# Three layers in one kernel on one core: the experts' second product is written with features as rows

## The chip, the cores and the metric

The kernel runs on one core of a Trainium2 chip. Its time is the device time of that core in microseconds (us). A core has five engines with queues of their own: PE (TensorE, the matrix array), DVE (VectorE), ACT (ScalarE), POOL (GpSimd) and SP (SyncE, which here only issues DMAs). Each works off its instructions in the order in which they were written; a wait on another engine holds up everything behind it on the same engine. PSUM, the memory that PE writes, has eight banks; one bank holds 128 rows of 512 float32.

## The reference

Three layers follow each other. Only the last is touched by the change.

```python
# 1. linear attention (4 batches, 8 heads, 768 steps, head width 48) -> x [3072, 384]
# 2. x = (h * tanh(softplus(h))) @ w_out,  h = x @ w_in        (384 -> 2048 -> 384), the "mish layer"
# 3. a mixture of 8 experts, all of them on every token:
P = exp(x @ w_gate - max)                 # [3072, 8], then 8 rounds of Sinkhorn scaling
for e in range(8):
    h = maximum(x @ w1[e], 0)             # 384 -> 1024
    out += P[:, e:e+1] * (h @ w2[e])      # 1024 -> 384
```

## The kernel before

Tokens are handled in 6 tiles of 512 (`n`), hidden features in chunks of 128 (`f`, 8 of them in an expert). A *unit* is one expert, one tile and one chunk; the experts have 8 x 6 x 8 = 384 units, and a loop passes over them with the expert outermost and the chunk innermost. To reach float32 accuracy at PE's fast rate, each operand is split into a high and a low fp32r part, and every product is taken three times (`PASSES`: high x high, high x low, low x high).

In a unit, `first(i)` (L254) makes the hidden chunk `ph`: 3 parts of x by 3 passes, 9 matmuls that each move 512 token columns past a 128x128 block of weights. `relu(i)` (L322 on ACT, L323 on DVE) turns `ph` into the two parts of `g`. `second_e(j)` (L364) multiplies by w2. Here a block of `g` (128 hidden features x 128 tokens) is loaded as the weights and 384 columns of w2 move: 4 blocks of tokens by 3 passes, 12 matmuls. The sums are four banks `ye`, one for each 128 tokens, with *tokens* as rows. In a loop iteration PE gets `first(i + 1)` and then `second_e(i - 2)`.

After a tile's eighth chunk, the four sums are added to the running result `acc` (L375, DVE, `scalar_tensor_tensor`): since tokens are rows, the expert's weight `P` is one number for each partition. With the last expert, four DMAs write the tile to `out` (L377). `first` products rotate over four PSUM banks (tag `h`), the sums over four others (`y0` to `y3`).

The mish layer before it has units too. There both products are written in the other form (L254 and `second_m`, L334): weights are loaded as weights, and 512 token columns of activations move, 9 matmuls and 9.

The order on every engine is the order of the Python calls (a manual schedule); SBUF and PSUM tiles come from pools that rotate, and an instruction that takes a slot waits for the last reader of the slot's holder before.

Of the kernel before, what the change touches and what calls it, by code (L numbers as in the profile page):

```python
# [21 lines left out]
NP = H // 2          # head pairs  # L22
DD = 2 * D           # columns of a pair
DR = 64 + D          # rows of a pair: the second head's begin at 64
C = 128              # chunk of the recurrence
NC = S // C
NTOK = B * S
DM = H * D           # 384
KI = DM // 128       # 3
TT = 512             # tokens of a tile  # L30
# [8 lines left out]
# square of the upper half of a float64 2^-126, read as a float32, by 2^30  # L39
TINY_SQ = 1.265625  # L40
H_MAX = 12.0
HUGE_SQ = 1.5e10     # no less than the square of the upper half of a float64 2^128
W_MIN, W_MAX = 0.6, 1.0625   # decays that the chunked form takes
ONE_BITS = 0x3F800000
PASSES = ((0, 0), (0, 1), (1, 0))
NWA = 24             # weight pieces of the lasting pool
# [6 lines left out]
NCA = 12             # weight pieces split beside the attention  # L53


@with_exitstack
def fused_kernel(ctx: ExitStack, tc: tile.TileContext, a, out):
    nc = tc.nc
    # the one activation table that holds both exp and ln
    nc.scalar.add_instruction(mybir.InstLoadActFuncSet(  # L60
        name=nc.get_next_instruction_name(), engine=mybir.EngineType.Activation, ins=[], outs=[],
        act_func_set_id=[t.name for t in SETS].index("natural_log_exp_and_others")))
    bad = ctx.enter_context(tc.tile_pool(name="bad", bufs=1)).tile([1, 1], F32, name="bad")
    layers(tc, a, out, bad, False)
    # decays or weights beyond the ranges that the chunked form and the conversion hold for
    with tc.If(nc.values_load(bad.bitcast(I32), min_val=0, max_val=ONE_BITS) > 0):
        layers(tc, a, out, None, True)
# [3 lines left out]
def layers(ctx: ExitStack, tc: tile.TileContext, a, out, bad, general):  # L71
# [9 lines left out]
    def bank(shape, nm, tag):  # L81
        """PSUM: four banks that rotate for first products, four for sums"""
        return ps.tile(shape, F32, name=nm, tag=tag, bufs=4 if tag == "h" else 1)
# [12 lines left out]
    wi, wo, rawn = {}, {}, []  # L96
    # the second product follows the first by some units, and so do its weights
# [17 lines left out]
    def conv_bits(m):  # L115
        """float64 weights, by their bits: the upper 21 bits of the value and the rest, in four steps"""
        load_raw(m + 1)
        lo, hi = rawn[m][:, :, 0], rawn[m][:, :, 1]
        v = mr.tile([128, DM], F32, name=f"v{m}", tag="v")
        q = mr.tile([128, DM], F32, name=f"q{m}", tag="q")  # L120
        parts[m] = v, q
        vb, qb = v.bitcast(U32), q.bitcast(U32)
        # exponent of 11 bits to 8: the top bit and the lower seven; sign, 20 bits of the fraction
        dve.tensor_scalar(vb, hi, 3, 0x3FFFFFFF, op0=ALU.logical_shift_left, op1=ALU.bitwise_and)  # L124
        yield
        dve.scalar_tensor_tensor(vb, hi, 0xC0000000, vb, op0=ALU.bitwise_and, op1=ALU.bitwise_or)  # L126
        yield
        if general:
            # below float32's normal range: zero; above: infinite
            sq = me.tile([128, DM], F32, name=f"sq{m}", tag="e", bufs=MB[0])  # L130
            act.activation(sq, hi.bitcast(F32), AF.Square)
            dve.scalar_tensor_tensor(v, sq, TINY_SQ * 2.0 ** -30, v, op0=ALU.is_ge, op1=ALU.mult)
            dve.tensor_scalar(sq, sq, HUGE_SQ, None, op0=ALU.is_lt)
            dve.reciprocal(sq, sq)
            dve.tensor_tensor(v, v, sq, op=ALU.mult)
        # the lower 32 bits of the fraction
        dve.tensor_scalar(qb, vb, 0xFF800000, None, op0=ALU.bitwise_and)  # L137
        yield
        dve.scalar_tensor_tensor(q, lo, 2.0 ** -52, q, op0=ALU.mult, op1=ALU.mult)  # L139
        yield  # L140

    def conv_act(m):
        # two exact fp32r parts of 24 bits in all
        w, f = wpieces[m]
        t = wA.tile([128, 2, KI, 128], F32R, name=f"wm{m}", tag="w")
        act.activation(t[:, 0].rearrange("p k f -> p (k f)"), parts[m][0], AF.Copy)
        (wi, wo)[w][f] = t
        load_raw(m + 3)
# [18 lines left out]
    def flag(m):  # L167
        # what lies outside float32's normal range leaves a mark
# [5 lines left out]
    # rings that the attention and the layers after it share  # L174
# [50 lines left out]
    # all tiles but the last see one half of the hidden features first, then the other,  # L225
    # so that the weights' parts can follow
# [8 lines left out]
    # weight pieces that are begun beside unit i  # L235
# [22 lines left out]
    def mish_e(i):  # L258
        # e = exp(min(h, H_MAX)), s = (e + 1)^2; beyond, tanh of the softplus is 1 in float32
# [10 lines left out]
    def mish_n(i):  # L270
        # tanh(log1p(e)) = e (e + 2) / (s + 1); what comes out is negative until the sums are taken
# [8 lines left out]
    def mish_r(i):  # L280
        # r = 1 / (s + 1), to be refined
# [6 lines left out]
    def mish_y(i):  # L288
        # ((s + 1) r - 2) r
# [66 lines left out]

    def second_e(j):
        e, n, f = units[j]
# [8 lines left out]
        if f == NF2 - 1:  # L367
            for s in range(NSUB):
                yo, o, gc = sums[n][s], acc[n][:, s, :], n * NSUB + s
                if e == 0:  # L370
                    act.activation(o, yo, AF.Copy)
                    continue
                if e == 1:
                    act.activation(o, o, AF.Copy, scale=Pm[:, gc, 0:1])
                dve.scalar_tensor_tensor(o, yo, Pm[:, gc, e:e + 1], o, op0=ALU.mult, op1=ALU.add)  # L375
                if e == E - 1:
                    nc.sync.dma_start(out[gc * 128:(gc + 1) * 128, :], o)  # L377

# [16 lines left out]
    def gate_out(n, pl):  # L395
        if not g32s or pl is not me:
            g32s.append(pl.tile([32, TT], F32, name=f"g32_{n}", tag="g32"))
            pool.memset(g32s[-1], 0.0)
        g32 = g32s[-1]
        act.activation(g32[0:2 * E, :], gate[n], AF.Copy)  # L400
        gt = pl.tile([32, TT // 32, 32], F32, name=f"gt{n}", tag="y", bufs=MB[3] if pl is me else 1)
        dve.transpose(gt.rearrange("p a b -> p (a b)"), g32)
        gv = gt.rearrange("p (s q) e -> p s q e", q=4)
# [43 lines left out]
    # what comes beside the units: splits of the next tile's x, the gate of a finished tile  # L447
# [21 lines left out]
    # ------------------------------------------------------------------  # L469
    # linear attention: chunks of 128 steps, head pairs stacked on partitions  # L470
    # ------------------------------------------------------------------
    last = []

    def chunked_attention(aw, ac):
# [36 lines left out]
        # power tables of w  # L511
        zero = ac.tile([DR, 1], F32, name="zero")
        pool.memset(zero, 0.0)
        Wr = ac.tile([DR, NP, C], F32, name="Wr")        # w^(j-64)
# [8 lines left out]
        # keeps the array busy, for its clock, until the first scores  # L523
# [3 lines left out]
        Wp = gpl.tile([DR, NP, 192], F32, name="Wp", tag="g")      # w^(j+1)  # L527
# [13 lines left out]
        Wk = ac.tile([DR, NP, C], F32, name="Wk")        # w^(63-j)  # L541
# [7 lines left out]
        def tables():  # L549
            powers(64, 192)  # L550
            Wh = me.tile([DR, NP, C], F32, name="Wh", tag="p", bufs=MB[2])        # w^(191-s)
# [28 lines left out]
        def a_q(i):  # L580
            # u term: b[s, h] = sum_d r u k
# [27 lines left out]
        def a_scores(i):  # L609
            x = T[i]  # L610
            # the two heads of a pair take their own rows of the array and banks
# [57 lines left out]
        def a_cv(i):  # L669
            # half a weight piece beside a unit  # L670
# [10 lines left out]
        # what each engine does while the scores of unit i are made, in its order  # L681
# [26 lines left out]
    def stepwise_attention(ac):  # L708
        """any w: the recurrence as it stands, for one column of the states of a head pair at a time"""
# [4 lines left out]
        # columns e and D + e of sel[:, D - 1 - e:] sum the rows of one head each  # L714
# [57 lines left out]
    with mst, tc.tile_pool(name="hf", bufs=1) as hf:  # L772
# [5 lines left out]
        for i in range(NM + 3):  # L778
            e, n, f = units[i]
            # the first product one unit ahead (two at the start), the second three behind  # L780
# [10 lines left out]
            # units i, i - 1 and i - 2, and between the steps on DVE the bits of a weight piece  # L791
# [42 lines left out]
    cp2 = ctx.enter_context(tc.tile_pool(name="cp2", bufs=1))  # L834
    sk = ctx.enter_context(tc.tile_pool(name="sk", bufs=1))
    acc = [cp2.tile([128, NSUB, DM], F32, name=f"acc{n}") for n in range(NT)]
# [6 lines left out]
    for i in range(NM + 3, NU + 2):  # L843
# [5 lines left out]
        if i < NU:  # L849
# [15 lines left out]
            if bad is not None and e == 2:  # L865
                # the mish layer's weights pass once more, beside the products, to be looked at
# [4 lines left out]
            if bad is not None and e == 3 and n == 0 and f == 2:  # L871
                # 1 for all that is in range; the least of every partition; are there 128 of them?
# [6 lines left out]
                dve.tensor_scalar(bad, okp, 127.5, None, op0=ALU.is_lt)  # L879
            if e == 0:  # L880
                if 0 <= m - 4 < KI:
# [17 lines left out]
def _lay_out(x):  # L899
# [8 lines left out]
    # rows of a head pair on the partitions: 48 of one head, 16 of none, 48 of the other  # L908
    def rows(z, fill=0):
        """z: [head of the pair, d, ...]"""  # L910
# [16 lines left out]
    # row of w_in that a partition of a feature chunk holds  # L927
# [26 lines left out]
```

## Time and profile before

| what | value |
|---|---|
| time, median of 3 runs | 2187.86 us (2185.88 to 2190.61) |
| the profiled execution: its span | 2188.3 us |
| PE busy | 2145.9 us, 98% |
| DVE, ACT, POOL busy | 911.3, 913.2 and 640.3 us |
| attention | about 0 to 155 us |
| mish layer | about 155 to 580 us |
| experts | 580 to 2183 us |

The profile is of one execution. "Busy" counts the time in which at least one instruction of the engine is in flight. PE's instructions overlap (a matmul is some 390 ns in flight, while the next starts 170 to 240 ns after it), so that the distance from start to start, not the duration, tells what a matmul costs. The rows that give this distance are those of the timeline: there neighbouring instructions of one line stand merged, with their count, and the next row's start tells when the group gave way.

### The profile page before, as it was taken

How to read it: one execution, taken by the hardware profiler on the slowest of the kernel's cores; microseconds unless marked ns; L12 is line 12 of the kernel's file. 1: busy time of each engine (PE TensorE's matmuls, PEld its weight loads, DVE VectorE, ACT ScalarE, POOL GpSimd, SP SyncE). 2: the span in 40 equal slices, each digit the busy share in tenths (PEclk: the TensorE clock that was granted, in tenths of full speed). 3: DMA queues.
4: the chain of work that ended last, by engine and by line, in shares of the span. 5: the costliest groups of instructions: out<-in, count | busy, mean ns of one | idle time of the engine just before them, and what ended most of it. 6: DMA issues, size and time to landing. Idle time of an engine off the chain costs nothing.

```text
span 2188.3 us, 27812 instructions
## 1 busy us (share of the span) xinstructions
PE 2145.9 (98%) x10974; PEld 1905.7 (87%) x10974; DVE 911.3 (42%) x1507; ACT 913.2 (42%) x1899; POOL 640.3 (29%) x550
## 2 busy tenths in 40 slices
PE   7889999999999999999999999999999999999998
PEld 7787777788889999999999999999999999999998
DVE  9999999999523322222212222222222122222222
ACT  6889898899522322244432122221311221221111
POOL 5546767655411211131013012211310131121100
PEclk8999999999999999999999999999999999999999
DMA  9640001000100100023311001000100010000000
GB/s 241 191 146 24 30 29 44 15 15 15 31 11 11 33 19 1 12 69 95 97 33 44 1 8 30 22 1 11 48 1 4 12 44 1 8 22 15 15 29 31
DMA packets 42204, 82.51 MB, mean 38 GB/s; under 512 B 5072, under 2 KB 28112, under 8 KB 42064
## 3 DMA queue, kind: packets, MB, share of 16 engines
q1 hardware_dynamic: 42064, 80.64, 12.6%
q8 instruction: 88, 1.44, 0.3%
q14 instruction: 52, 0.43, 0.1%
HBM read 75.91 MB, written 4.72 MB: 37 GB/s over the span
## 4 chain that ended last, share of the span: by engine, by line
PE 85%; DVE 7%; ACT 3%; issue 2%; DMA 1%; POOL 1%; SPq 0%; DVEq 0%; ACTq 0%; POOLq 0%
PE ph L254 41%; PE ye L364 37%; PE x L334 5%; DVE q L137 1%; DVE ph L273 1%; DVE y L292 1%; PE ya L656 1%; DVE q L139 1%; DMA ld<-in_rkT_dram 1%; DVE pn L276 1%; ACT A L607 1%; DMA lt<-in_kr_dram 1%; DVE v L126 0%; DVE y L295 0%; PE ya L654 0%
## 5 line engine op out<-in xcount | busy, mean ns | idle before, releaser
L364 PE MATMUL ye<-we,g 128*128 128x384 f32 x4608 | 869.9, 337 | 0.0
L254 PE MATMUL ph<-xs,we 128*128 128x512 f32 x3456 | 861.9, 393 | 0.0
L364 PEld LDWEIGHTS ye<-we,g 128*128 128x128 f32 x4608 | 819.1, 188 | 34.1 <-DVE xT L350 0.5
L254 PEld LDWEIGHTS ph<-xs,we 128*128 128x128 f32 x3456 | 642.4, 188 | 117.9 <-issue 0.2
L322 ACT ACTIVATE g<-ph 128x512 fp32r<-128x512 f32 x384 | 229.7, 600 | 1137.2 <-PE ye L364 1132.3
L323 DVE SCALAR_TENSOR_TENSOR g<-ph,g 128x512 fp32r<-128x512 f32 x384 | 260.9, 688 | 975.5 <-ACT g L322 975.4
L196 POOL TENSOR_TENSOR xs<-xT,xs 128x512 fp32r<-128x512 f32 x177 | 227.6, 1295 | 866.5 <-ACT xs L195 866.5
L221 POOL TENSOR_TENSOR we<-er,we 128x384 fp32r<-128x384 f32 x118 | 117.7, 1015 | 414.7 <-ACT we L220 414.7
L334 PE MATMUL x<-g,wm 128*128 128x512 f32 x864 | 216.5, 392 | 7.8 <-POOL g L317 7.6
L254 PE MATMUL ph<-xs,wm 128*128 128x512 f32 x864 | 211.9, 390 | 0.6 <-POOL xs L196 0.6
L334 PEld LDWEIGHTS x<-g,wm 128*128 128x128 f32 x864 | 160.5, 188 | 48.3 <-POOL g L317 14.2
L254 PEld LDWEIGHTS ph<-xs,wm 128*128 128x128 f32 x864 | 161.9, 188 | 36.7 <-POOL xs L196 1.1
L375 DVE SCALAR_TENSOR_TENSOR acc<-ye,Pm,acc 128x384 f32<-128x384 f32 x168 | 92.8, 613 | 228.1 <-PE ye L364 228.1
L317 POOL TENSOR_TENSOR g<-y,g 128x512 fp32r<-128x512 f32 x96 | 124.3, 1295 | 134.9 <-ACT g L312 130.8
L195 ACT ACTIVATE xs<-xT 128x512 fp32r<-128x512 f32 x177 | 105.3, 622 | 0.0
L261 ACT ACTIVATE e<-ph,lim 128x512 f32<-128x512 f32 x96 | 65.7, 684 | 35.5 <-DVE pn L276 30.2
L273 DVE TENSOR_TENSOR ph<-ph,e 128x512 f32<-128x512 f32 x96 | 66.6, 694 | 17.2 <-ACT e L263 17.0
L263 ACT ACTIVATE e<-e,lim 128x512 f32<-128x512 f32 x96 | 68.5, 714 | 0.0
L276 DVE SCALAR_TENSOR_TENSOR pn<-e,ph 128x512 f32<-128x512 f32 x96 | 65.8, 685 | 4.3 <-DVE v L124 0.2
L292 DVE SCALAR_TENSOR_TENSOR y<-sq,ph 128x512 f32<-128x512 f32 x96 | 65.2, 679 | 0.0
L656 PE MATMUL ya<-A,vz 128*96 128x128 f32 x384 | 63.4, 298 | 0.0
L220 ACT ACTIVATE we<-er 128x384 fp32r<-128x384 f32 x128 | 61.6, 515 | 1.0 <-DMA er<-in_w_dram 1.0
(118 smaller groups left out, 1295.1 us busy)
## 6 DMA issues: line engine op xcount, KB each, us to landing
er<-in_w_dram SPq DMA_DIRECT2D x128, 192.0 KB, 2.4
ld<-in_rkT_dram SPq DMA_DIRECT2D x24, 448.0 KB, 5.5
lt<-in_kr_dram SPq DMA_DIRECT2D x24, 384.0 KB, 5.8
raw<-in_w_in_dram SPq DMA_DIRECT2D x16, 384.0 KB, 3.1
raw<-in_w_out_dram SPq DMA_DIRECT2D x16, 384.0 KB, 3.0
seen<-in_w_in_dram SPq DMA_DIRECT2D x16, 384.0 KB, 3.1
seen<-in_w_out_dram SPq DMA_DIRECT2D x16, 384.0 KB, 3.0
lv<-in_v_dram SPq DMA_DIRECT2D x24, 192.0 KB, 3.1
```

The lines of the kernel that those rows point to most:

```text
L195: act.activation(xs[:, 0, :], xT[n][:, k, :], AF.Copy)
L196: eng.tensor_tensor(xs[:, 1, :], xT[n][:, k, :], xs[:, 0, :].bitcast(F32), op=ALU.subtract)
L221: eng.tensor_tensor(tl, raw, th.bitcast(F32), op=ALU.subtract)
L254: pe.matmul(ph, w[:, pw, k, :], xs[:, px, :], start=(m == 0), stop=(m == 3 * KI - 1))
L273: dve.tensor_tensor(ph, ph, e, op=ALU.mult)
L276: dve.scalar_tensor_tensor(pn, e, 2.0, ph, op0=ALU.add, op1=ALU.mult)
L317: pool.tensor_tensor(gs[i][:, 1], y, gs[i][:, 0].bitcast(F32), op=ALU.subtract)
L322: act.activation(g[:, 0], ph, AF.Relu)
L323: dve.scalar_tensor_tensor(g[:, 1], ph, 0.0, g[:, 0].bitcast(F32), op0=ALU.max, op1=ALU.subtract)
L334: pe.matmul(sums[n][k], wo[f][:, pw, k, :], g[:, px, :], start=(f == f0 and m == 0), stop=(f == f1 and m == 2))
L364: pe.matmul(sums[n][s], g[:, px, s * 128:(s + 1) * 128], w2[e, f][:, pw].rearrange("p k f -> p (k f)"), start=(f == 0 and m == 0), stop=(f ...
L375: dve.scalar_tensor_tensor(o, yo, Pm[:, gc, e:e + 1], o, op0=ALU.mult, op1=ALU.add)
```

## The change

The second product of the experts takes the form of the mish layer, in 47 of the 48 pairs of expert and tile: blocks of w2 are the weights, 512 columns of `g` move, 3 blocks of output features by 3 passes, 9 matmuls. The sums are three banks with *features* as rows (they rotate over the four banks). Now P differs along the columns. So P is turned once (`p_rows`, two matmuls with the identity), written to DRAM (`prow`), and for every expert and tile 512 values of it are read back into all 128 partitions (`load_p`, tile `pb`).

At the end of a tile, DVE multiplies a sum by `pb` into `t`, and POOL adds `t` to `acc`, three times. (For the second expert POOL also scales `acc` by the first expert's `pb`.) With the last expert each finished third of `acc` is turned in blocks of 32x32 on DVE and goes to `out` in 12 DMAs of 64 KB, whose pieces are 128 bytes.

The last expert's last tile stays in the old form (`second_t`). For it, `acc` of that tile is turned to tokens as rows by 12 matmuls (`turn`), four times three, one group in each of four units of the tile before. A helper of the gate also shares a buffer differently; the remaining differences are comments.

```diff
     def second_e(j):
         e, n, f = units[j]
+        if (e, n) == TOKJ:
+            return second_t(j)
         if f == 0:
-            sums[n] = [bank([128, DM], f"ye{e}_{n}_{s}", f"y{s}") for s in range(NSUB)]
+            sums[n] = [bank([128, TT], f"ye{e}_{n}_{k}", f"y{(ycnt[0] + k) % 4}") for k in range(KI)]
+            ycnt[0] += KI
         g = gs.pop(j)
-        for s in range(NSUB):
+        for k in range(KI):
             for m, (pw, px) in enumerate(PASSES):
-                pe.matmul(sums[n][s], g[:, px, s * 128:(s + 1) * 128],
-                          w2[e, f][:, pw].rearrange("p k f -> p (k f)"),
+                pe.matmul(sums[n][k], w2[e, f][:, pw, k, :], g[:, px, :],
                           start=(f == 0 and m == 0), stop=(f == NF2 - 1 and m == 2))
         if f == NF2 - 1:
-            for s in range(NSUB):
-                yo, o, gc = sums[n][s], acc[n][:, s, :], n * NSUB + s
+            for k in range(KI):
+                yo, o = sums[n][k], acc[n][:, k, :]
...
                 if e == 1:
-                    act.activation(o, o, AF.Copy, scale=Pm[:, gc, 0:1])
-                dve.scalar_tensor_tensor(o, yo, Pm[:, gc, e:e + 1], o, op0=ALU.mult, op1=ALU.add)
+                    pool.tensor_tensor(o, o, pb[0, n], op=ALU.mult)
+                t = tt[:, k % 2, :]
+                dve.tensor_tensor(t, yo, pb[e, n], op=ALU.mult)
+                pool.tensor_tensor(o, o, t, op=ALU.add)
                 if e == E - 1:
-                    nc.sync.dma_start(out[gc * 128:(gc + 1) * 128, :], o)
+                    dve.transpose(xT[n][:, k, :], o)
+                    ot = xT[n][:, k, :].rearrange("p (a b) -> p a b", b=32)
+                    ov = out[n * TT:(n + 1) * TT, :].rearrange("(b i) d -> i b d", i=32)
+                    for a4 in range(4):
+                        c0 = k * 128 + a4 * 32
+                        nc.sync.dma_start(ov[:, :, c0:c0 + 32], ot[32 * a4:32 * a4 + 32])
...
+    def turn(s):
+        tp = bank([128, DM], f"tp{s}", "h")
+        for k in range(KI):
+            pe.matmul(tp[:, k * 128:(k + 1) * 128], acc[NT - 1][:, k, s * 128:(s + 1) * 128], unit,
+                      start=True, stop=True)
+        act.activation(accT[:, s, :], tp, AF.Copy)
...
+    def load_p(e, n):
...
+        nc.sync.dma_start(pb[e, n], prow[n * NSUB:(n + 1) * NSUB, e, :].unsqueeze(0).to_broadcast([128, NSUB, 128]))
...
+            if e > 0 and f == 2:
+                if e == 1:
+                    load_p(0, n)
+                load_p(e, n)
+            if e == E - 1 and n == NT - 2 and 0 <= f - 2 < NSUB:
+                turn(f - 2)
             if e == 0:
+                if m == 46:
+                    p_rows()
```

PE's order at the end of the last expert's tile 3, before: `ye` is a bank of sums (tile, block), `ph` a first product, `we` a piece of weights, `g` its parts; the last number only tells buffers apart.

```order
L364 MATMUL ye_3_3_16683<-we_15790,g_16746 128x384 x3
L254 MATMUL ph_16808<-xs_4_0_16774,we_14554 128x512 x3
L254 MATMUL ph_16808<-xs_4_1_16802,we_14554 128x512 x3
L254 MATMUL ph_16808<-xs_4_2_16805,we_14554 128x512 x3
L364 MATMUL ye_3_0_16680<-we_15825,g_16771 128x384 x3
L364 MATMUL ye_3_1_16681<-we_15825,g_16771 128x384 x3
L364 MATMUL ye_3_2_16682<-we_15825,g_16771 128x384 x3
L364 MATMUL ye_3_3_16683<-we_15825,g_16771 128x384 x3
L254 MATMUL ph_16833<-xs_4_0_16774,we_14589 128x512 x3
```

PE's order where the last expert's tile 3 ends and tile 4 begins, after the change (`tp` is a bank of `turn`):

```order
L371 MATMUL ye_3_0_15797<-g_15930,we_15047 128x512 x3
L371 MATMUL ye_3_1_15798<-g_15930,we_15047 128x512 x3
L371 MATMUL ye_3_2_15799<-g_15930,we_15047 128x512 x3
L254 MATMUL ph_15999<-xs_4_0_15880,we_14764 128x512 x3
L254 MATMUL ph_15999<-xs_4_1_15905,we_14764 128x512 x3
L254 MATMUL ph_15999<-xs_4_2_15908,we_14764 128x512 x3
L371 MATMUL ye_4_0_16009<-g_15952,we_13827 128x512 x3
L371 MATMUL ye_4_1_16010<-g_15952,we_13827 128x512 x3
L371 MATMUL ye_4_2_16011<-g_15952,we_13827 128x512 x3
L401 MATMUL tp_16026<-unit,acc_6003 128x128 x3
L254 MATMUL ph_16031<-xs_4_0_15880,we_14947 128x512 x3
```

Four groups of three with 384 columns became three groups of three with 512, as wide as those of `first`, and a `turn` stands between a second product and the next first.

DVE's order at the end of the last expert's first tile, before. In brackets stand the engines that an instruction waits for; `g` is what L323 makes of a first product `ph`:

```order
L375 SCALAR_TENSOR_TENSOR acc_5992<-ye_0_0_16017,Pm,acc_5992 128x384 [waits PE_49]
L375 SCALAR_TENSOR_TENSOR acc_5992<-ye_0_1_16018,Pm,acc_5992 128x384 [waits PE_49]
L375 SCALAR_TENSOR_TENSOR acc_5992<-ye_0_2_16019,Pm,acc_5992 128x384 [waits PE_49]
L375 SCALAR_TENSOR_TENSOR acc_5992<-ye_0_3_16020,Pm,acc_5992 128x384 [waits PE_49]
L323 SCALAR_TENSOR_TENSOR g_16225<-ph_16170,g_16225 128x512 [waits Activation_49]
```

DVE's order at the end of the last expert's second tile, after the change (`t` is the product with `pb`, `xT` what is turned of `acc`):

```order
L384 TENSOR_TENSOR t_1_15550<-ye_1_0_15373,pb_1_15388 128x512 [waits DMAHW0_49,PE_49]
L388 STREAM_TRANSPOSE xT_75<-acc_5999 128x512 [waits Pool_49]
L384 TENSOR_TENSOR t_1_15550<-ye_1_1_15374,pb_1_15388 128x512 [waits PE_49]
L388 STREAM_TRANSPOSE xT_75<-acc_5999 128x512 [waits Pool_49]
L384 TENSOR_TENSOR t_1_15550<-ye_1_2_15375,pb_1_15388 128x512 [waits DVE_49,PE_49]
L388 STREAM_TRANSPOSE xT_75<-acc_5999 128x512 [waits Pool_49]
L323 SCALAR_TENSOR_TENSOR g_15572<-ph_15509,g_15572 128x512 [waits Activation_49]
```

Each turning waits for POOL's add, which waits for the product ahead of it, and the next unit's `g` (L323) stands behind all six.

## Rows read from the trace of the kernel before

**Rows 1.** The page's first part: busy us, share of the span, instructions.

```profile
PE 2145.9 (98%) x10974; PEld 1905.7 (87%) x10974; DVE 911.3 (42%) x1507; ACT 913.2 (42%) x1899; POOL 640.3 (29%) x550
```

**Rows 2.** The chain that ended last, share of the span by engine.

```profile
PE 85%; DVE 7%; ACT 3%; issue 2%; DMA 1%; POOL 1%; SPq 0%; DVEq 0%; ACTq 0%; POOLq 0%
```

**Rows 3.** Groups by line: names, form, count | busy us, mean ns | idle before.

```profile
L364 PE MATMUL ye<-we,g 128*128 128x384 f32 x4608 | 869.9, 337 | 0.0
L254 PE MATMUL ph<-xs,we 128*128 128x512 f32 x3456 | 861.9, 393 | 0.0
```

**Rows 4.** Windows (mish, experts): PE, PEld, DVE, ACT, POOL busy, clock, DMA share, GB/s.

```profile
200.00:400.00 200.00, 195.05 (x845) 157.24 (x845) 187.35 (x279) 177.78 (x327) 142.66 (x113) 1.00 0.10 31
1200.00:1400.00 200.00, 200.00 (x1004) 181.15 (x1003) 45.30 (x72) 44.71 (x82) 38.77 (x34) 1.00 0.06 17
```

**Rows 5.** Timeline of PE in the experts, one tile long: start, us, what.

```profile
1382.60 2.27 PE L364 MATMUL ye<-we,g 128*128 128x384 f32 x12
1384.70 2.24 PE L254 MATMUL ph<-xs,we 128*128 128x512 f32 x9
...
1416.09 2.27 PE L364 MATMUL ye<-we,g 128*128 128x384 f32 x12
```

**Rows 6.** Timeline of PE in the mish layer, three units.

```profile
201.19 2.20 PE L334 MATMUL x<-g,wm 128*128 128x512 f32 x9
203.23 2.20 PE L254 MATMUL ph<-xs,wm 128*128 128x512 f32 x9
...
213.43 2.20 PE L334 MATMUL x<-g,wm 128*128 128x512 f32 x9
```

**Rows 7.** Timeline of PE just behind the gate's narrow matmuls.

```profile
561.93 2.23 PE L254 MATMUL ph<-xs,we 128*128 128x512 f32 x9
564.00 2.20 PE L334 MATMUL x<-g,wm 128*128 128x512 f32 x9
566.04 2.20 PE L254 MATMUL ph<-xs,we 128*128 128x512 f32 x9
```

**Rows 8.** Groups by line: the operations nearest to the new ones.

```profile
L350 DVE TENSOR_TENSOR xT<-half,x 128x512 f32<-128x512 f32 x15 | 10.1, 681 | 2.0 <-PE x L334 2.0
L402 DVE STREAM_TRANSPOSE gt<-g 32x512 f32<-32x512 f32 x6 | 4.1, 691 | 0.5 <-ACT g L400 0.5
L196 POOL TENSOR_TENSOR xs<-xT,xs 128x512 fp32r<-128x512 f32 x177 | 227.6, 1295 | 866.5 <-ACT xs L195 866.5
L307 POOL TENSOR_TENSOR y<-y,pn 128x512 f32<-128x512 f32 x32 | 46.8, 1463 | 7.7 <-DVE y L295 5.5
```

**Rows 9.** Timeline of DVE at the end of a tile.

```profile
1416.81 2.21 DVE L375 SCALAR_TENSOR_TENSOR acc<-ye,Pm,acc 128x384 f32<-128x384 f32 x4 [5.47 <-PE ye L364]
1418.94 1.28 DVE L323 SCALAR_TENSOR_TENSOR g<-ph,g 128x512 fp32r<-128x512 f32 x2
```

**Rows 10.** Timeline of POOL and PE where PE waits for POOL.

```profile
288.84 1.28 POOL L317 TENSOR_TENSOR g<-y,g 128x512 fp32r<-128x512 f32 x1
290.18 1.21 PE L334 MATMUL x<-g,wm 128*128 128x512 f32 x4 [0.77 <-POOL g L317]
```

**Rows 11.** Timeline of POOL in the experts.

```profile
1572.80 3.95 POOL L221 TENSOR_TENSOR we<-er,we 128x384 fp32r<-128x384 f32 x4
1599.61 1.29 POOL L196 TENSOR_TENSOR xs<-xT,xs 128x512 fp32r<-128x512 f32 x1 [22.87 <-ACT xs L195]
```

**Rows 12.** Timeline of PE in the attention: float32 matmuls of 128 columns.

```profile
108.14 0.60 PE L656 MATMUL ya<-A,vz 128*96 128x128 f32 x4
108.58 0.38 PE L654 MATMUL ya<-rt,st 112*96 112x128 f32 x2
```

**Rows 13.** Timeline of SP: its last issues.

```profile
2181.51 1.97 SPq L377 DMA_DIRECT2D out_dram<-acc  x4
```

**Rows 14.** DMA issues: names, count, KB each, median us to landing.

```profile
out_dram<-acc SPq DMA_DIRECT2D x24, 192.0 KB, 1.9
...
unit<-in_ident_dram SPq DMA_DIRECT2D x1, 64.0 KB, 1.7
```

More of the change, by code (lines that the diff above doesn't have):

```diff
@@ L355, in evac_m, with second_t @@
             yield
+    ycnt = [0]
+    TOKJ = (E - 1, NT - 1)
     def second_e(j):
+        e, n, f = units[j]
+        if (e, n) == TOKJ:
+            return second_t(j)
+        if f == 0:
+            sums[n] = [bank([128, TT], f"ye{e}_{n}_{k}", f"y{(ycnt[0] + k) % 4}") for k in range(KI)]
+            ycnt[0] += KI
+        g = gs.pop(j)
+        for k in range(KI):
+            for m, (pw, px) in enumerate(PASSES):
+                pe.matmul(sums[n][k], w2[e, f][:, pw, k, :], g[:, px, :],
+                          start=(f == 0 and m == 0), stop=(f == NF2 - 1 and m == 2))
+        if f == NF2 - 1:
+            if e > 0:
+                tt = sk.tile([128, 2, TT], F32, name=f"t{e}_{n}", tag="g")
+            for k in range(KI):
+                yo, o = sums[n][k], acc[n][:, k, :]
+                if e == 0:
+                    act.activation(o, yo, AF.Copy)
+                    continue
+                if e == 1:
[3 more added lines that the diff above has]
+                pool.tensor_tensor(o, o, t, op=ALU.add)
+                if e == E - 1:
+                    dve.transpose(xT[n][:, k, :], o)
[4 more added lines that the diff above has]
+                        nc.sync.dma_start(ov[:, :, c0:c0 + 32], ot[32 * a4:32 * a4 + 32])
+    accT = xT[0].rearrange("p k t -> p (k t)").rearrange("p (s d) -> p s d", s=NSUB)
+    def turn(s):
[4 more added lines that the diff above has]
+        act.activation(accT[:, s, :], tp, AF.Copy)
+    def second_t(j):
         e, n, f = units[j]
@@ L368, in second_e, with p_rows @@
             for s in range(NSUB):
-                yo, o, gc = sums[n][s], acc[n][:, s, :], n * NSUB + s
[L370 to L373, printed above, removed]
-                    act.activation(o, o, AF.Copy, scale=Pm[:, gc, 0:1])
-                dve.scalar_tensor_tensor(o, yo, Pm[:, gc, e:e + 1], o, op0=ALU.mult, op1=ALU.add)
-                if e == E - 1:
-                    nc.sync.dma_start(out[gc * 128:(gc + 1) * 128, :], o)
+                o, gc = accT[:, s, :], n * NSUB + s
+                dve.scalar_tensor_tensor(o, sums[n][s], Pm[:, gc, e:e + 1], o, op0=ALU.mult, op1=ALU.add)
+                nc.sync.dma_start(out[gc * 128:(gc + 1) * 128, :], o)
+    pb = {}
+    HS = NS // 2
+    def p_rows():
+        pt = sk.tile([HS * E, 2, 128], F32, name="pt", tag="g")
+        for i in range(2):
+            tp = bank([HS * E, 128], f"ptp{i}", "h")
+            pe.matmul(tp, Pm[:, i * HS:(i + 1) * HS, :].rearrange("p s e -> p (s e)"), unit, start=True, stop=True)
+            act.activation(pt[:, i, :], tp, AF.Copy)
+            nc.sync.dma_start(prow[i * HS:(i + 1) * HS].rearrange("s e t -> (s e) t"), pt[:, i, :])
+    def load_p(e, n):
+        if (e, n) == TOKJ:
+            return
+        pb[e, n] = pbp.tile([128, NSUB, 128], F32, name=f"pb{e}_{n}", tag="pb")
+        nc.sync.dma_start(pb[e, n], prow[n * NSUB:(n + 1) * NSUB, e, :].unsqueeze(0).to_broadcast([128, NSUB, 128]))
+        pb[e, n] = pb[e, n].rearrange("p s t -> p (s t)")
     gate, g32s = {}, []
@@ L395, in gate_out @@
     def gate_out(n, pl):
[L396 to L399, printed above, removed]
+        if pl is me:
+            if not g32s:
+                g32s.append(pl.tile([32, TT], F32, name="g32", tag="g32"))
+                pool.memset(g32s[0], 0.0)
+            g32 = g32s[0]
+            gt = pl.tile([32, TT], F32, name=f"gt{n}", tag="y", bufs=MB[3])
+        else:
+            both = pl.tile([32, 2, TT], F32, name=f"gt{n}", tag="g")
+            g32, gt = both[:, 0, :], both[:, 1, :]
+            pool.memset(g32, 0.0)
         act.activation(g32[0:2 * E, :], gate[n], AF.Copy)
-        gt = pl.tile([32, TT // 32, 32], F32, name=f"gt{n}", tag="y", bufs=MB[3] if pl is me else 1)
-        dve.transpose(gt.rearrange("p a b -> p (a b)"), g32)
-        gv = gt.rearrange("p (s q) e -> p s q e", q=4)
+        dve.transpose(gt, g32)
+        gv = gt.rearrange("p (s q e) -> p s q e", q=4, e=32)
         for q in range(4):
@@ L835, in layers @@
     sk = ctx.enter_context(tc.tile_pool(name="sk", bufs=1))
-    acc = [cp2.tile([128, NSUB, DM], F32, name=f"acc{n}") for n in range(NT)]
+    pbp = ctx.enter_context(tc.tile_pool(name="pbp", bufs=3))
+    dr = ctx.enter_context(tc.tile_pool(name="dr", bufs=1, space=bass.MemoryType.DRAM))
+    prow = dr.tile([NS, E, 128], F32, name="prow")
+    acc = [cp2.tile([128, KI, TT], F32, name=f"acc{n}") for n in range(NT)]
     ones = cp2.tile([128, 128], F32, name="ones")
@@ L879, in layers @@
                 dve.tensor_scalar(bad, okp, 127.5, None, op0=ALU.is_lt)
+            if e > 0 and f == 2:
+                if e == 1:
+                    load_p(0, n)
+                load_p(e, n)
+            if e == E - 1 and n == NT - 2 and 0 <= f - 2 < NSUB:
+                turn(f - 2)
             if e == 0:
+                if m == 46:
+                    p_rows()
                 if 0 <= m - 4 < KI:
```

## Prediction, made before the changed kernel ran

> **What bounds the kernel now.** I read the page's busy shares first. PE is busy 98% of the span and the other engines under half [rows 1], and the chain of work that ended last runs over PE for 85% [rows 2]. Time is therefore won or lost only by what a matmul costs on PE, or by making PE wait. The groups by line name the two that matter: the experts' first and second products hold PE for 861.9 and 869.9 us [rows 3]. Their mean durations (393 and 337 ns) are no price, since matmuls overlap. The windows tell that PE never idles among the experts (200.00 of 200 us, granted clock 1.00, which is the 2.4 GHz level), while in the mish layer it idles at times at the same clock [rows 4].
>
> The price is in the timeline, from start to start. Among the experts the same group comes back after 8 units at 1416.09 - 1382.60 = 33.49 us, so a unit takes 4.186 us: 2.10 for the 12 matmuls of 384 columns and 2.08 for the 9 of 512 [rows 5]. In the mish layer, where both products move 512 columns, three units take 213.43 - 201.19 = 12.24 us: 4.080 each, 2.04 for either nine [rows 6]. L254 is the same code in both stages, at the same clock, from the same pools, yet costs 2.08 here and 2.04 there. What differs is its neighbour. At 561.93 the first product follows a gate matmul, whose loaded block is 16 columns wide; these nine take 2.07 us, and the next nines 2.04 again [rows 7]. So I read the excess as a disturbance that a change of shape leaves in PE's pipeline and that fades over some matmuls; among the experts every unit has two such changes.
>
> **The change part by part.**
>
> *Pace of PE.* With 9 + 9 matmuls of 512, an expert unit is what a mish unit is now, in operands, split and order. I take 4.080 us: 4.186 - 4.080 = 0.106 us for a unit, times 47 x 8 = 376 units, is -39.9 us. Only some of this is a column effect (9 x 512 = 12 x 384 columns); it hangs on the shape no longer changing. Bounds: if the second product only takes the first one's present 2.08, a unit is 4.16 and the gain 376 x 0.026 = 9.8 us; if columns alone counted, nothing. I choose the mish rows because they show this very stream, with the other engines busier than here.
>
> The Trainium skill ("TensorE: Matmul & The Clock Gate", section "Back-to-back issue gap") says that a matmul of N columns costs N / 2.4 GHz plus about 2.5 ns, whatever its neighbours. By that a unit saves only three times 2.5 ns, 2.8 us over the 376 units (an estimate from that page). The trace does not agree with it: 2.04 us for nine is 227 ns each, 13 ns over the column time, and the nines of one line differ by stage.
>
> *End of a tile, experts 1 to 6.* Before, four DVE operations of together 2.21 us stand ahead of the next `g` [rows 9]. Now it is three products (0.68 us each, as the subtraction of a bank in L350 [rows 8]), and the third waits until POOL's first add has freed half of `t`. Counting from the end of the tile's last second product: the first sum's last matmul starts 7 x 0.227 = 1.59 us earlier and is some 0.39 in flight [rows 3], so that DVE begins at about -1.15; product to -0.46; POOL's add, 1.30 us as L196 [rows 8], with 0.06 us for a handoff each way (290.12 to 290.18 [rows 10]) to +0.96; third product to 1.7; `g` to 2.4 us. PE first needs the low part of this `g` after three products of 2.04 and one matmul, at 6.35. So 4 us to spare, hidden. The scaling by POOL with expert 1 can run ahead of the sum. The next tile takes the free fourth bank first, and the two that it takes next are released at -0.46 and +0.2, before PE comes to them. POOL is idle for over 20 us at a time, and its burst between experts is over long before the next tile ends [rows 11].
>
> *End of a tile, last expert, five times.* Here the six operations of DVE run in series with POOL's three adds: per third 0.69 (product) + 0.06 + 1.30 (add) + 0.06 + 0.69 (turning, the 691 ns of a 32x512 one, since its length along a row is the same [rows 8]) = 2.80. Three of them from -1.15 end at 7.25, `g` at 7.94. PE wants it at 6.35: it waits 1.6 us. Three of the five ends cost this. At the end of tile 3 the first `turn` takes one of the four `h` banks, and the first product behind it needs the bank of just the `ph` whose `g` is late: PE is there at 2.04 + 2.04 + 0.65 = 4.7 and waits 3.2. At the end of tile 4 the last tile wants all four `y` banks; its first is the one that the third product frees, at -1.15 + 2 x 2.80 + 0.69 = 5.1, and PE is there at 2.04: 3.1 us. Sum 3 x 1.6 + 3.2 + 3.1 = +11.1 us. Bounds: were the adds hidden, 0; with adds of 1.46 us (L307 [rows 8]) and handoffs of 0.2 a third takes 0.44 more, 1.3 for an end, +17.5 in all. A wait this short leaves the clock alone: in the mish layer waits of 0.77 us recur [rows 10] at clock 1.00 [rows 4].
>
> *Added matmuls.* A float32 matmul of 128 columns is two records of 0.11 us (four in 108.58 - 108.14 = 0.44 [rows 12]). `turn` has 12, `p_rows` two: 28 records, 3.1 us. Each of these five insertions, and each restart, leaves nine matmuls some 0.03 to 0.05 us longer [rows 7], 0.4 together. Sum +3.5 us.
>
> *DMAs.* 47 loads of P of 256 KB have 7 units, 28 us, until they are used; DMAs of 192 and 64 KB land in 1.9 and 1.7 us [rows 14]. The 60 writes of the last expert each have 512 pieces of 128 bytes, which this trace does not show. From above: in the experts' window 0.06 of 16 engines for 200 us moved 17 GB/s, mostly weights in pieces of 1536 bytes (384 float32), so about 0.087 us a piece [rows 4]; at that price a write is 32 pieces on each of 16 engines, 2.8 us, and twelve 33 us, just a tile's time; the last twelve begin some 24 us before PE's end (8 units of 4.19 less 2.04, less the 7.25 of DVE's chain) and would end the kernel 10 us later. From below, in proportion to the bytes, 3 us, hidden. Issuing takes SP 0.5 us each [rows 13], 6 for twelve. I take the lower end, since a piece has a twelfth of the bytes. The kernel's end is in the old form, as it was.
>
> *Sum*, against the profiled execution: 2188.3 - 39.9 + 11.1 + 3.5 = 2163.0 us. That span is 0.4 us above the median of the runs, so no correction is made.
>
> **Rivals.**
>
> *Columns decide.* The excess among the experts has another cause than the change of shape, and stays. Then the gain is between 0 and 9.8 us and the added 14.6 us remain: 2193 to 2203, slower. For it: the equal column counts. Against it: [rows 5 to 7]. By the rule of the Trainium skill above it would be 2188.3 - 2.8 + 14.6 = 2200. It wins as soon as the unit stays above 4.147 us.
>
> *Every tile end stalls.* If POOL comes to its first add over 4 us late, DVE holds the next `g` in 42 tiles instead of 5; each microsecond beyond costs 37 more, and 0.7 us eat the gain: 2188 and slower. Against it: POOL's idle time [rows 11].
>
> *Small pieces choke the queue.* Then the last expert's writes end after PE: 2163 + 10 = 2173, more if a piece of 128 bytes is dearer than one of 1536.
>
> *The pace is half won*, for some other disturbance keeps nines between 2.04 and 2.08: 2188.3 - 25 + 14.6 = 2178.
>
> **How the numbers follow.** The forecast, 2163, has 0.72; the half-won pace and the small pieces 0.08 each; columns 0.07; tile ends 0.05. The range reaches down to no stalls at all (2188.3 - 39.9 + 3.5 = 2152, less one) and up to the half-won pace with a little on top: 2151 to 2180. About 0.2% (4 us) is what a measurement of this kernel can tell from no change: slower, 0.10, takes the columns and most of the tile ends; the same, 0.05, the rest of these and some of the small pieces; faster by more is what is left, 0.85.
>
> **What would show it.** In the profile after: the same group of a second product 32.64 us later in a tile of experts 1 to 6, nines of 2.04; PE idle time before the second product of the last expert, released by DVE, about 1.6 us three times and 3 us twice; no PE wait at the other tile ends; the old form's tail unchanged. I am wrong if nines stay at 2.08, if PE waits on DVE in every tile, or if the last event is a DMA of the turned tiles.

## The result and the profile after

The changed kernel takes 2164.52 us (median of 4 runs, 2160.97 to 2165.99), the kernel before 2188.66 beside it: a ratio of 0.9888, 95% interval 0.9874 to 0.9902, so 24 us or 1.1% faster. 2163 was forecast. The profiled execution has a span of 2161.7 us.

The page of the changed kernel, busy shares and the two products (columns as in [rows 1] and [rows 3]):

```profile
PE 2108.2 (98%) x9874; PEld 1749.2 (81%) x9874; DVE 914.4 (42%) x1481; ACT 902.2 (42%) x1875; POOL 820.5 (38%) x691
...
L254 PE MATMUL ph<-xs,we 128*128 128x512 f32 x3456 | 848.0, 390 | 2.7 <-DVE g L323 2.7
L371 PE MATMUL ye<-g,we 128*128 128x512 f32 x3384 | 829.0, 389 | 3.5 <-DVE g L323 3.5
```

PE has 1100 instructions less and is still busy 98%. L254 lost 14 us of busy time although its instructions are the same. POOL gained 180 us, for the adds and the second expert's scalings. In the experts DVE waits for it, and the DMA queue as before; of PE only one weight load does, for 0.3 us in the second expert.

The timeline of PE over one tile, changed kernel (start, us, what), which answers to [rows 5]:

```profile
1385.33 2.20 PE L371 MATMUL ye<-g,we 128*128 128x512 f32 x9
1387.37 2.20 PE L254 MATMUL ph<-xs,we 128*128 128x512 f32 x9
...
1417.97 2.20 PE L371 MATMUL ye<-g,we 128*128 128x512 f32 x9
```

The same group comes back after 32.64 us, where it was 33.49: each nine takes 2.04 us, as in the mish layer [rows 6].

Who made PE wait between 570 us and the end, changed kernel (us in total, times, longest):

```profile
PE ye L371 <- DVE g L323: 3.5, 3, 1.2
PE ye L412 <- DVE t L384: 2.8, 1, 2.8
PE ph L254 <- DVE g L323: 2.7, 1, 2.7
```

These are five waits, all at tile ends of the last expert. At the other 42 tile ends in the new form PE is not idle (six of the 42 are the first expert's, where no product with P is taken). The timeline of the first of the five, DVE, POOL and PE:

```profile
1981.95 0.69 DVE L384 TENSOR_TENSOR t<-ye,pb 128x512 f32<-128x512 f32 x1 [5.53 <-PE ye L371]
...
1984.67 0.65 DVE L384 TENSOR_TENSOR t<-ye,pb 128x512 f32<-128x512 f32 x1
...
1985.40 1.29 POOL L385 TENSOR_TENSOR acc<-acc,t 128x512 f32<-128x512 f32 x1 [1.40 <-DVE t L384]
1986.72 0.71 DVE L388 STREAM_TRANSPOSE xT<-acc 128x512 f32<-128x512 f32 x1 [1.40 <-POOL acc L385]
...
1987.36 0.65 DVE L384 TENSOR_TENSOR t<-ye,pb 128x512 f32<-128x512 f32 x1
1988.09 1.29 POOL L385 TENSOR_TENSOR acc<-acc,t 128x512 f32<-128x512 f32 x1 [1.40 <-DVE t L384]
...
1989.42 0.71 DVE L388 STREAM_TRANSPOSE xT<-acc 128x512 f32<-128x512 f32 x1 [1.40 <-POOL acc L385]
1990.05 1.85 DVE L323 SCALAR_TENSOR_TENSOR g<-ph,g 128x512 fp32r<-128x512 f32 x3
...
1990.76 2.12 PE L371 MATMUL ye<-g,we 128*128 128x512 f32 x8 [1.20 <-DVE g L323]
```

DVE and POOL hand each third to and fro (2.69 us from product to product, 1984.67 to 1987.36), the first of three `g` behind them ends at about 1990.7, 8.7 us after the first product began (1981.95), and PE starts with it at 1990.76.

The timeline of PE at the last two of the five waits, changed kernel:

```profile
2089.45 0.83 PE L401 MATMUL tp<-unit,acc 128*128 128x128 f32 x6
2093.00 2.33 PE L254 MATMUL ph<-xs,we 128*128 128x512 f32 x9 [2.72 <-DVE g L323]
...
2128.89 3.89 PE L412 MATMUL ye<-we,g 128*128 128x384 f32 x12 [2.83 <-DVE t L384]
2132.61 0.63 PE L254 MATMUL ph<-xs,we 128*128 128x512 f32 x2
```

The windows around the last one (columns as in [rows 4]):

```profile
2128.00:2133.00 5.00, 4.11 (x14) 4.10 (x15) 2.62 (x5) 0.19 (x1) 1.27 (x1) 0.66 0.62 98
```

Twelve matmuls of 384 columns need 3.72 us there (2128.89 to 2132.61) instead of 2.10: the granted clock is 0.66 over these 5 us, a mixture of the two levels. Nine of the twelve stand 320 ns apart, which for 384 columns is 1.2 GHz.

DMAs of the changed kernel (KB each, us to landing), answering to [rows 14]:

```profile
pb<-prow SPq DMA_DIRECT2D x47, 256.0 KB, 5.4
...
out_dram<-xT SPq DMA_DIRECT2D x60, 64.0 KB, 2.0
```

### The profile page after: what moved, and what is told of

Read it like the earlier page. It is cut to its first block, busy times and chain, and to the rows that moved or that the text cites. A ratio compares the mean times of both kernels' runs of the same rounds, so it can differ in the third digit from the quotient of the medians.

```text
span 2161.7 us, 25851 instructions
## 1 busy us (share of the span) xinstructions
PE 2108.2 (98%) x9874; PEld 1749.2 (81%) x9874; DVE 914.4 (42%) x1481; ACT 902.2 (42%) x1875; POOL 820.5 (38%) x691
## 5 line engine op out<-in xcount | busy, mean ns | idle before, releaser
L254 PE MATMUL ph<-xs,we 128*128 128x512 f32 x3456 | 848.0, 390 | 2.7 <-DVE g L323 2.7
L371 PE MATMUL ye<-g,we 128*128 128x512 f32 x3384 | 829.0, 389 | 3.5 <-DVE g L323 3.5
L254 PEld LDWEIGHTS ph<-xs,we 128*128 128x128 f32 x3456 | 647.5, 188 | 137.5 <-DVE g L323 2.9
L371 PEld LDWEIGHTS ye<-g,we 128*128 128x128 f32 x3384 | 635.0, 188 | 136.9 <-DVE g L323 4.8
L323 DVE SCALAR_TENSOR_TENSOR g<-ph,g 128x512 fp32r<-128x512 f32 x384 | 260.4, 688 | 900.9 <-ACT g L322 900.7
L385 POOL TENSOR_TENSOR acc<-acc,t 128x512 f32<-128x512 f32 x123 | 156.3, 1293 | 451.0 <-DVE t L384 448.6
L254 PE MATMUL ph<-xs,wm 128*128 128x512 f32 x864 | 212.2, 390 | 0.8 <-POOL xs L196 0.8
L254 PEld LDWEIGHTS ph<-xs,wm 128*128 128x128 f32 x864 | 161.9, 188 | 37.2 <-POOL xs L196 1.2
L384 DVE TENSOR_TENSOR t<-ye,pb 128x512 f32<-128x512 f32 x123 | 82.2, 688 | 254.9 <-PE ye L371 226.7
```

What stands on the lines that cost most here:

```text
L254: pe.matmul(ph, w[:, pw, k, :], xs[:, px, :], start=(m == 0), stop=(m == 3 * KI - 1))
L323: dve.scalar_tensor_tensor(g[:, 1], ph, 0.0, g[:, 0].bitcast(F32), op0=ALU.max, op1=ALU.subtract)
L371: pe.matmul(sums[n][k], w2[e, f][:, pw, k, :], g[:, px, :], start=(f == 0 and m == 0), stop=(f == NF2 - 1 and m == 2))
L384: dve.tensor_tensor(t, yo, pb[e, n], op=ALU.mult)
L385: pool.tensor_tensor(o, o, t, op=ALU.add)
```

## The experiments

**The changed kernel again**, for comparison on the same chip.

> The changed kernel as it is, run beside the others for comparison. All theories: 2164 us, 1.1% under the kernel before.

Measured: 2165.32 us (2162.51 to 2166.44), ratio 0.9896 (0.9881 to 0.9912); PE has the same five waits. The result repeats.

**Is it the shape that changes, or the roles?** The old roles, 512 columns instead of 384:

```diff
...
-                          w2[e, f][:, pw].rearrange("p k f -> p (k f)"),
+                          w2[e, f].rearrange("p w k f -> p (w k f)")[:, 256 * pw:256 * pw + TT],
...
```

> Kernel before, with its second product in the old roles (blocks of g as weights, w2 moving), but 512 columns moving instead of 384: 128 columns of the neighbouring part of w2 go along into an unused part of the bank, and for the low part of w2 the columns are shifted, so the sums are not the reference's. The order and the count of instructions are those of before. Theory (a change of shape disturbs PE's stream, whatever the roles): nothing changes shape any more, so the first product's nines fall from 2.08 to 2.04 us although nothing was done to them, the twelves take 12 x 0.2267 = 2.72, a unit 4.76, the kernel 2188 + 384 x 0.574 = 2408 us. Rival (the roles matter: g as weights, or w2 as the moving operand, disturbs the stream): nines stay at 2.08, twelves at 12 x 0.231 or more, a unit at 4.85 or more, the kernel 2443. Rival (columns alone): nines stay at 2.08, twelves 12 x 0.234 = 2.81 by the old cost of a column, a unit 4.88.

Measured: 2408.77 us (one run). The timeline of PE:

```profile
1402.69 2.20 PE L254 MATMUL ph<-xs,we 128*128 128x512 f32 x9
1404.73 2.88 PE L364 MATMUL ye<-we,g 128*128 128x512 f32 x12
1407.45 2.20 PE L254 MATMUL ph<-xs,we 128*128 128x512 f32 x9
```

The nine matmuls of a first product start 2.04 us before the next group, not 2.08, though nothing was done to them; the twelve take 2.72, a unit 4.76. With `g` still as the weights the stream is as smooth as after the change. So the roles do not matter, nor the count of instructions; both rivals are out by over 30 us.

**Does a change of shape disturb the new form?** One matmul of nine cut in two:

```diff
+                if (k, m) == (1, 1):
+                    for c in (0, TT // 2):
+                        pe.matmul(sums[n][k][:, c:c + TT // 2], w2[e, f][:, pw, k, :], g[:, px, c:c + TT // 2],
+                                  start=False, stop=False)
+                    continue
```

> Changed kernel, with one of the nine matmuls of each second product of the new form (the middle one) cut into two of 256 columns: the same weights, columns and result. Theory (each matmul costs its columns plus 13 ns, and a change of shape disturbs the ones behind it): a unit grows by 0.013 us for the extra matmul and by 0.03 to 0.07 us of disturbance, to 4.12 to 4.16 us; the kernel by 17 to 30 us, to about 2187; the nines of the first product behind it, untouched, go above 2.04. Rival (only the number of matmuls counts, the disturbance belongs to the old form): a unit 4.093, the kernel 5 us longer, the first product's nines at 2.04.

Measured: 2176.79 us (2174.05 to 2177.68), ratio to before 0.9946 (0.9931 to 0.9962), 11.5 us more than the changed kernel beside it. The timeline of PE:

```profile
1402.37 1.07 PE L376 MATMUL ye<-g,we 128*128 128x512 f32 x4
1403.27 0.40 PE L373 MATMUL ye<-g,we 128*128 128x256 f32 x2
1403.51 1.09 PE L376 MATMUL ye<-g,we 128*128 128x512 f32 x4
1404.44 2.21 PE L254 MATMUL ph<-xs,we 128*128 128x512 f32 x9
1406.48 1.07 PE L376 MATMUL ye<-g,we 128*128 128x512 f32 x4
```

The two halves take 0.233 us (1403.273 to 1403.506 unrounded), 0.006 more than one whole, where the theory had put 0.013. The four untouched matmuls behind them take 0.930 us where four at 0.2267 take 0.907, and the first of the next nine is slower too, by 0.004; the other eight are not, so that these nine take 2.04 to two digits, as the rival had it. A unit is 4.11 us (1402.37 to 1406.48), 0.033 above the changed kernel's: 0.006 for one more matmul and 0.027 of disturbance. The disturbance is there in the new form, against the rival's 5 us; but the size was missed, 11.5 us for a forecast of 17 to 30. A single narrow place disturbs five matmuls behind it, a little less than I had read from the gate [rows 7].

**Half as many changes of shape, with the old instructions.** The order of PE alone, from the second expert on:

```diff
-        if i + 1 < NU:
-            first(i + 1)
-        second_e(i - 2)
...
+        elif (i - NM) % 2:
+            for j in (i + 1, i + 2):
+                if j < NU:
+                    first(j)
+            for j in (i - 2, i - 1):
+                if j < NU:
+                    second_e(j)
...
```

> Kernel before, every instruction as it was, but from the second expert on PE gets two first products in a row and then two second products (9, 9, 12, 12 matmuls instead of 9, 12, 9, 12), so the shape changes half as often. Theory (the change of shape disturbs, and the disturbance fades over some matmuls): of a pair of units' excess of 0.13 us about half goes; 0.05 to 0.07 us for each of 168 pairs, 8 to 11 us less than before, near 2178. Rival (the disturbance belongs to a matmul of the old form or to its columns, wherever it stands): 2188, no change. A third outcome, new waits of PE for g, would show as idle time of PE and make it slower.

Measured: 2194.09 us (2191.27 to 2201.68), ratio 1.0033 (1.0022 to 1.0045): slower, the third of the outcomes named, with another releaser than the one named. The timeline of PE:

```profile
1404.63 4.70 PE L254 MATMUL ph<-xs,we 128*128 128x512 f32 x18
1409.17 4.35 PE L364 MATMUL ye<-we,g 128*128 128x384 f32 x24
1413.35 4.28 PE L254 MATMUL ph<-xs,we 128*128 128x512 f32 x18
1417.47 4.35 PE L364 MATMUL ye<-we,g 128*128 128x384 f32 x24
...
```

The waits of PE's weight loads between 800 and 2180 us, same kernel:

```profile
PEld ph L254 <- POOL xs L196: 23.4, 41, 0.6
```

A clean pair takes 8.30 us (1409.17 to 1417.47), two units before 8.37. But at nearly every tile end the eighteen take some 0.4 us more, as here 4.54 (1404.63 to 1409.17): the second of the two first products now comes earlier, and POOL's last part of the next x is late. 41 such waits take more than the pairs won. So the same kernel with x split one unit earlier (`f in (4, 5)` for `(5, 6)`):

> The pairing of e2_pair (9, 9, 12, 12 matmuls), with the parts of the next tile's x made one unit earlier, since there PE waited 0.4 us for POOL's last part at nearly every tile end. Theory: the waits go, 0.066 us stays won in each of 168 pairs, 11 us less than before, near 2177 (0.995). Rival (the pairing wins nothing, what the clean pairs won is lost elsewhere): 2188.

Measured: 2177.46 us (2174.59 to 2180.49), ratio 0.995 (0.9938 to 0.9963), as forecast. The timeline of PE, with no wait left at a tile's end:

```profile
1407.41 4.28 PE L254 MATMUL ph<-xs,we 128*128 128x512 f32 x18
1411.53 4.35 PE L364 MATMUL ye<-we,g 128*128 128x384 f32 x24
1415.71 4.28 PE L254 MATMUL ph<-xs,we 128*128 128x512 f32 x18
```

No matmul was changed, added or taken away, and 11 us went with half of the changes of shape.

**The waits of the last expert.** The turnings are put behind the next `g`:

```diff
                 if e == E - 1:
-                    dve.transpose(xT[n][:, k, :], o)
...
+                    late.append((n, k, o))
...
             relu(i)
+            turned()        # the transposes of `late` and their DMAs
```

> Changed kernel, but the three turnings of a finished tile (and their writes) stand on DVE behind the next unit's g instead of between the products. Theory (the five waits of PE in the last expert come from DVE's serial chain of product, POOL's add and turning, and the slow clock behind the longest one comes from that wait): PE's waits of 1.4, 1.4, 1.4, 2.7 and 2.8 us, 1.5 us of matmuls at half pace and some 0.3 us of disturbance go, 11 to 12 us less than the changed kernel, near 2153; the clock stays at full speed; no PE wait on DVE in the last expert. Rival (the wait only moves: turnings behind g delay the g after it, or the writes come too late for the last tile): less than 5 us won, with a new wait of PE on DVE or ACT one or two units later.

Measured: 2153.51 us (2150.91 to 2155.16), ratio to before 0.984 (0.9827 to 0.9854), 11.8 us below the changed kernel beside it. DVE's timeline at the end of the last expert's first tile:

```profile
1984.33 1.31 DVE L384 TENSOR_TENSOR t<-ye,pb 128x512 f32<-128x512 f32 x2 [5.54 <-PE ye L371]
1986.43 0.69 DVE L384 TENSOR_TENSOR t<-ye,pb 128x512 f32<-128x512 f32 x1 [0.78 <-POOL acc L385]
1987.04 0.68 DVE L323 SCALAR_TENSOR_TENSOR g<-ph,g 128x512 fp32r<-128x512 f32 x1
1987.63 2.01 DVE L394 STREAM_TRANSPOSE xT<-acc 128x512 f32<-128x512 f32 x3
```

And the window over the last expert's later part, same kernel:

```profile
1980.00:2150.00 170.00, 166.17 (x766) 140.38 (x764) 48.00 (x73) 31.09 (x55) 34.33 (x27) 1.00 0.20 35
```

`g` ends 3.4 us after the first product with `pb` began instead of 8.7, PE waits for nobody among the experts, and the clock stays at 1.00. This version beats both kernels. As a base for the next run it was taken once more:

> The changed kernel with the turnings behind the next g once more, as the base of the run beside it: 2153 to 2154.

Measured: 2151.71 us (2150.38 to 2156.27), ratio 0.9841 (0.9827 to 0.9855).

**The old form at the very end.** In that version, the last tile in the new form as well (`TOKJ = None`, no `turn`):

> As that one, and the last expert's last tile in the new form too (no old form at the end, no turn matmuls). Theory: PE saves 8 x 0.106 us of pace and four turns of 0.58 us with 0.13 of disturbance each, 3.7 together; the end grows, since behind PE's last matmul there are now product, POOL's add, turning and 12 issues of 0.5 us instead of the last scalar_tensor_tensor and its DMA: DVE ends some 4.3 us after PE instead of 0.7, SP issues until 6 us after PE, 5 together. Net +1 to +2: 2154 to 2156. Rival (the old form at the end is worth nothing or costs): 2150, 3 less.

Measured: 2156.65 us (2153.71 to 2157.72), 4.9 us more than the run beside it. The sign was right, the size was not. Timeline of the end, same kernel (PE, then DVE and SP):

```profile
2134.15 8.32 PE L371 MATMUL ye<-g,we 128*128 128x512 f32 x36
```

```profile
2143.84 1.33 DVE L394 STREAM_TRANSPOSE xT<-acc 128x512 f32<-128x512 f32 x2
2144.56 6.67 SPq L399 DMA_DIRECT2D out_dram<-xT  x12
2145.67 0.71 DVE L394 STREAM_TRANSPOSE xT<-acc 128x512 f32<-128x512 f32 x1 [0.51 <-POOL acc L385]
```

From the first second product to the last matmul the experts take 1562.7 us, 3.2 less than in the run beside it, near the 3.7 expected. But the kernel ends 13.4 us after that matmul, not 6.1: SP issues until 2151.23, 8.8 us after PE, where I had put 6. The issues begin only 2.1 us behind PE's last matmul, when the first third is turned, and the twelve take 6.7.

## Why the prediction was right

*Pace of PE.* Forecast -39.9 us from 4.080 us a unit; where nothing else enters the stream, the units take 4.080 us to the last digit. The reason holds too, shown from three sides: wide columns in the old roles smooth the stream, a cut in the new form disturbs it, and halving the changes of shape wins 11 us. In the first and the last of these L254 changes its pace, though none of its instructions is changed. The gain of a unit, 0.107 us, can now be divided: settled matmuls cost their columns plus 13.3 ns (227 ns for 512; 173.3 for 384, as the second twelve of a pair in e3_pair_xs show; at clock 1.00), so three fewer are 0.040 us, and the disturbance, gone, was the other 0.067.

The Trainium skill ("TensorE: Matmul & The Clock Gate", section "Back-to-back issue gap") gives the formula behind the 2.8 us as the gap of an isolated matmul, a condition that the prediction left out. For a stream of matmuls with weight loads the same section of the Trainium skill gives about 131 ns at 512 columns. The trace agrees with neither: settled matmuls of 512 stand 227 ns apart, 13.3 over the columns, and the neighbours count.

*Tile ends, experts 1 to 6.* Hidden, as forecast; PE is idle at none of them.

*Tile ends, last expert.* Forecast 3 x 1.6 + 3.2 + 3.1 = 11.1. The five waits in the profile are idle time, 9.0 us together, counted from the end of a matmul that is itself 0.39 us in flight. From start to start, which is how the prediction counted, PE is 1.36, 1.31, 1.31, 2.88 and 3.00 us late (behind the first wait 1.585 from one start to the next, where 0.227 is usual): 9.9. Place, count and releaser were right, the sizes 1.2 too large. The chain was 2.69 us a third instead of 2.80, mostly since DVE starts an instruction some 0.08 us before the one ahead of it ends, and the three thirds add up.

*What was missing.* That the longest wait would be followed by the lower clock: I had read from waits of 0.77 us that short ones are not. Behind it twelve matmuls took 1.6 us more. And restarts cost more than the 0.03 to 0.05 us put down for each: behind the first wait the matmuls lose 0.15 us before they are settled. In all the tile ends cost 12.0 us, by the experts' time with and without them (1577.8 in the changed kernel, 1565.8 in e1_late, whose median is 11.8 lower). That 11.1 came so near is luck: waits too long by 1.2 stood against 2.1 of slow clock and restarts that the term did not have.

*Added matmuls.* Forecast 3.5; four `turn`s of 0.59 us (2097.21 to 2097.80 in the trace) with 0.13 behind each, and 0.36 for `p_rows` with 0.11 behind, are 3.3. Here too two errors cancel: the matmuls are 2.7 instead of 3.1, and what they leave behind is 0.13 each instead of 0.03 to 0.05.

*DMAs.* I took the lower end, and it is right: 512 pieces of 128 bytes land in 2.0 us, and each tile's twelve were through long before the next came. By the trace's DMA records such a piece takes 12 ns of its DMA engine, against the 87 of the upper end. The loads of P take 5.4 us of the 28 they have. The 0.5 us for an issue was misread and came true by luck: the four issues of [rows 13] take SP 0.33 to 0.46 us each and stand 0.5 apart because each waits for its `acc` on DVE, which takes that long. An issue of one of the new writes does take SP 0.5 us; that shows where SP is waited for, at the end of e2_late_none.

*The sum.* From the first second product to the last matmul the experts took 1601.9 us before and 1577.8 after: -24.1, where -25.3 was forecast. With 12.0 for the tile ends and 3.3 for the added matmuls, 39.4 are left for the pace, 0.5 less than forecast. The rest of the 26.6 us between the two profiled spans lies before the experts, whose start differs by as much between executions without any change (576.7 and 580.4 us in two of the same kernel, e2_late and e1_late).

## What to carry to other kernels

Read a matmul's price from start to start, and compare the same line in two stages of one kernel: where it costs more, look at its neighbours. A dense stream of matmuls of one shape is cheaper than one that alternates between two shapes with the same columns in all, and grouping equal shapes wins without touching any instruction, if the inputs are there in time. When a finished tile passes to and fro between two engines, put everything that can wait behind the next unit's input.

## What the runs showed of the hardware

A disturbance by a change of shape lasts: behind 384 columns the nine matmuls of 512 stay uneven to the last (223 to 237 ns, 231 on average for 227), behind 512 the first six of 384 are uneven (171 to 185 ns), then 173.3; in e3_pair_xs the second nine of eighteen are at 227 again. What in PE causes it is not shown by any run.

A wait of 2.8 us of PE was followed by nine matmuls of 384 columns 320 ns apart, at 1.2 GHz, in three executions with that wait (after, e1_again, e1_split); one of 2.7 us in the same executions was followed by none. What else decided it, the runs don't tell.
